# Two attention-fed MoE layers on one Trainium2 core: converting float64 weights with two VectorE operations, an in-place rebias and three load buffers

## The chip, the cores and the metric

The kernel runs on one core of a Trainium2 chip. Its five engines work side by side, each on its own in-order list of instructions: TensorE (PE in the profile; its weight loads are PEld), VectorE (DVE), ScalarE (ACT), GpSimd (POOL), and SyncE (SP), which here only issues transfers. The metric is the device time of one execution in microseconds, as a median over runs.

## The reference, cut to what matters

Attention over 4 batches of 576 tokens, 8 heads of 64: a pooled part (four neighbouring tokens averaged) plus a banded part. Its output x (2304 tokens by 512) goes through two MoE layers. The weights of both layers arrive as float64.

```
x   = attention(q, k, v)                                  # float32
x   = (sigmoid(x @ w_gate) * (x @ w_val)) @ w_out         # MoE 1: 512 -> 1536 -> 512
h   = x @ w2_in                                           # MoE 2: 512 -> 2048 -> 512
out = (h * tanh(log(1 + exp(h)))) @ w2_out                # float32
```

## The kernel before

The program treats the four batches in turn. While TensorE multiplies batch b in MoE 1 (`m1` and `m1out`, lines 846 and 875), the attention of batch b+1 is woven in between, so all engines have work of both. MoE 2 follows for all tokens at the end.

**Weights.** MoE 1 has 18 units of weights (12 for the first products, 6 for the second), each fetched in two halves of 128 x 512 float64 words. They are converted once, in the block of batch 0, written to DRAM as float32 (`wd`, lines 228 and 256), and read back from there for batches 1 to 3. One half goes through these steps:

- `load64` (line 169): SyncE issues the load of the raw words (512 KB) into a `raw` tile of 128 x 512 x 2 int32. There are two `raw` buffers.
- `narrow` (line 176): a double's high word is read as a float32 and rebiased by ScalarE (line 178) into a tile of its own, `rebias` (two buffers of 128 x 512). VectorE then has three operations: shift that left by three (line 180, one source), OR in the top three bits of the low word (line 181, two sources), OR in the sign (line 185, two sources).
- `split` (line 189): ScalarE rounds the float32 to float32r (line 190), and GpSimd, or VectorE in some places, subtracts to get the rest (line 191). TensorE multiplies with both parts.

`d`, the float32 tile, holds a whole unit and has two buffers.

**What orders the work.** The first batch's attention, with the first three units, is written out by hand in `ORDER`, where `wf`, `wn` and `ws` are fetch, narrow and split of a half. All later steps are laid by `weave` (line 792) on a modelled TensorE clock: a step is emitted once those it depends on lie far enough back. In block 0 the fetch of half (u, x) depends on the narrowing of (u - 1, x), two halves before (line 271). The narrowing `wp` (line 242, `part`) comes at least 6000 ns of that clock after its fetch, and at least 2100 ns after the half before. The matmuls' slots need the splits of their unit, and a unit needs its place in a ring of three.

MoE 2's weights pass through `narrow` too: 16 halves of `w2_out` (`narrow_steps`, blocks 1 and 2) and 16 of `w2_in` (block 3). In MoE 2 itself the activation (`mish_a`) keeps its tile `e` in the `raw` buffers, and the output (`finish`, line 1097) passes through the `rebias` buffers.

Of the kernel before, what the change touches and what calls it, by code (L numbers as in the profile page):

```python
# [8 lines left out]
F32 = mybir.dt.float32  # L9
F32R = mybir.dt.float32r  # L10
I32 = mybir.dt.int32
AF = mybir.ActivationFunctionType
# [5 lines left out]
# the first batch's loads and steps in the order of their issue  # L18
ORDER = [['k0a', 'k0c', 'k1a', 'k1c', 'q0a', 'q0c', 'v1a', 'v1c', 'w0', 'q1c', 'v0c', 'w2', 'v0a',
# [11 lines left out]
# the engines of those steps, and how far apart the second batch's steps are laid (ns)  # L31
# [17 lines left out]
def attn_moe_kernel(  # L49
# [30 lines left out]
    T2 = 256  # L80
# [5 lines left out]
    def subs(b):  # L86
        """The two parts of the tokens of batch b that the products of MoE 1 take in turn."""
        a = 2 * TQ if b == 0 else SUB
        return slice(0, a), slice(a, S)
# [10 lines left out]
    class Step:  # L100
        """A piece of a program: what emits it, the time it takes of the tensor engine, and
        what has to lie how far back on the tensor engine's clock."""
# [5 lines left out]
    # ---------------------------------------------------------------- memory  # L108
# [21 lines left out]
    # the products of MoE 1 come to lie where the first batch's rows are gone  # L130
# [37 lines left out]
    # ------------------------------------------------- float64 words to float32  # L168
    def load64(src, n):
        r = fpool.tile([128, 512, 2], I32, tag="raw", name="raw")  # L170
        SP.dma_start(
            out=r.rearrange("p (a b) z -> p a (b z)", a=n), in_=src.bitcast(I32)
        )
        return r

    def narrow(r, d):
        g = fpool.tile([128, 512], F32, tag="rebias", name="rebias")
        ACT.activation(out=g, in_=r[:, :, 1].bitcast(F32), func=AF.Copy, scale=2.0 ** -112)  # L178
        gi, di = g.bitcast(I32), d.bitcast(I32)
        DVE.tensor_scalar(out=di, in0=gi, scalar1=3, scalar2=None, op0=ALU.logical_shift_left)  # L180
        DVE.scalar_tensor_tensor(  # L181
            out=di, in0=r[:, :, 0], scalar=29, in1=di,
            op0=ALU.logical_shift_right, op1=ALU.bitwise_or,
        )
        DVE.scalar_tensor_tensor(  # L185
            out=di, in0=gi, scalar=SIGN, in1=di, op0=ALU.bitwise_and, op1=ALU.bitwise_or
        )
# [5 lines left out]
    # ------------------------------------------------------- weights of MoE 1  # L193
# [15 lines left out]
    def weights(b):  # L209
        """The steps that bring the units of block b on chip and split them."""  # L210
# [52 lines left out]
        for u in range(NU1):  # L263
            for x in range(2):
# [5 lines left out]
                if b == 0:  # L270
                    deps = [(("wp", b, u - 1, x), 0.0)]
# [15 lines left out]
    # ------------------------------------------------------------- attention  # L287
# [3 lines left out]
    def windows(i):  # L291
        """Of tile i: first query, first key, first row used and rows used, for its halves."""
# [8 lines left out]
    def attention(b):  # L301
# [43 lines left out]
        # the first batch's rows lie where the products of MoE 1 come later, four neighbouring  # L345
        # tokens of half the sequence to a partition
# [110 lines left out]
        # pooled attention, half the queries at a time; heads in the order (parity, pair)  # L457
# [39 lines left out]
        # the same for half of the pairs, with the transposes  # L497
# [68 lines left out]
        # banded attention, two windows of 64 queries by 64 keys at a time  # L566
# [225 lines left out]
    def weave(slots, steps):  # L792
        """Emits the slots in their order, and the steps among them: each once what it stands
        on lies far enough back, and the paced ones evenly by cost."""
# [44 lines left out]
    # ----------------------------------------------------------------- MoE 1  # L839
# [6 lines left out]
    def m1(b, f, sub):  # L846
# [14 lines left out]
        # sigmoid(a) = (1 + tanh(a / 2)) / 2; the last half comes with the second product  # L861
# [13 lines left out]
    def m1out(b, c2, fg, j, ps):  # L875
# [19 lines left out]
        if fg == last_g:  # L895
            if b == B - 1 and c2:
                # the ring is free but for its last unit
# [12 lines left out]
    def block(b, extra):  # L910
        """MoE 1 of batch b with the steps of `extra` woven in."""
# [29 lines left out]
    # ------------------------------------------------------- weights of MoE 2  # L941
# [224 lines left out]
```

## Time and profile before

| what | value |
| --- | --- |
| runs | 1068.31, 1070.77, 4706.45 us; median 1070.77 us |
| span of the profiled execution, first to last instruction | 1069.6 us |
| what the median has beyond that span | 1.2 us |
| TensorE busy | 1023.1 us (96%) |
| VectorE busy | 690.6 us (65%) |
| ScalarE busy | 521.3 us (49%) |
| GpSimd busy | 195.2 us (18%) |
| mean granted TensorE clock | 0.987 of full |

The profile gives no time of the profiled execution other than its span; it lies between the two lowest runs. A share of busy time is a mean over stages with different limits: here the first 300 us (attention of batch 0, block 0, start of block 1) differ from the rest. A TensorE that is busy is not one at its peak, since matmuls overlap and the granted clock may be low.

### The profile page before, as it was taken

The numbers are of one execution on the slowest core, as the hardware profiler recorded it, in microseconds if no ns is written. First come the engines' busy times: TensorE is split into PE (matmuls) and PEld (weight loads), VectorE is DVE, ScalarE is ACT, GpSimd is POOL, SyncE is SP. The second block draws the span as 40 slices with busy tenths as digits, with TensorE's granted clock in tenths as the row PEclk, the third lists the DMA queues.
The fourth block names the chain that finished last, engine by engine and source line by source line (L and its number), as shares of the span: only waits on it lengthen the run. The fifth ranks groups of instructions, "written<-read, shape, count | busy, mean of one in ns | idle before, by whom it ended". The sixth has DMA issues, their size and how long they took to land.

```text
span 1069.6 us, 20453 instructions
## 1 busy us (share of the span) xinstructions
PE 1023.1 (96%) x8152; PEld 956.0 (89%) x8152; DVE 690.6 (65%) x1107; ACT 521.3 (49%) x1222; POOL 195.2 (18%) x235
## 2 busy tenths in 40 slices
PE   4698988999999999999999999999999999999998
PEld 3588978899999999899999999999999999999997
DVE  6977988856975537955488931867555555555552
ACT  4654657346665437565356631654443443433432
POOL 6456564630400400400000002000000000000000
PEclk9998998999999999999999999999999999999999
DMA  8639665777752457622375548212112020220001
GB/s 199 174 103 238 178 204 189 220 241 237 220 184 60 135 179 227 212 101 61 124 243 182 173 167 264 65 29 59 23 37 60 1 60 5 56 60 1 21 1 40
DMA packets 122240, 134.51 MB, mean 126 GB/s; under 512 B 54432, under 2 KB 99488, under 8 KB 122144
## 3 DMA queue, kind: packets, MB, share of 16 engines
q1 hardware_dynamic: 110336, 115.37, 35.1%
q0 software_dynamic: 11808, 17.83, 6.2%
q8 instruction: 64, 1.05, 0.4%
q14 instruction: 32, 0.26, 0.1%
HBM read 101.19 MB, written 31.98 MB: 124 GB/s over the span
## 4 chain that ended last, share of the span: by engine, by line
PE 77%; DVE 11%; DMA 6%; ACT 3%; issue 2%; SPq 0%; POOL 0%; DVEq 0%; ACTq 0%
PE ps_m L857 7%; PE ps_m L859 7%; PE ps_m L858 7%; PE h L1060 6%; PE h L1062 6%; PE h L1061 6%; PE po L1070 6%; PE po L1068 6%; PE po L1069 6%; PE ps_o L888 5%; PE ps_o L890 4%; PE ps_o L892 4%; DVE d L181 2%; DMA raw<-in_moe_w_out_dram 2%; DVE d L185 2%
## 5 line engine op out<-in xcount | busy, mean ns | idle before, releaser
L857 PE MATMUL ps_m<-R 128*128 128x288 f32 (+2 forms) x768 | 236.0, 309 | 4.2 <-DVE sg L863 4.2
L858 PE MATMUL ps_m<-R 128*128 128x288 f32 (+2 forms) x768 | 232.5, 303 | 0.8 <-POOL R L191 0.8
L859 PE MATMUL ps_m<-R 128*128 128x288 f32 (+2 forms) x768 | 232.7, 303 | 0.5 <-POOL R L191 0.5
L857 PEld LDWEIGHTS ps_m<-R 128*128 128x128 f32 x768 | 148.4, 194 | 9.6 <-DVE sg L863 4.6
L190 ACT CAST R<-d 128x512 fp32r<-128x512 f32 (+1 forms) x192 | 108.6, 583 | 89.2 <-PE ps_o L890 34.4
L858 PEld LDWEIGHTS ps_m<-R 128*128 128x128 f32 x768 | 148.8, 194 | 1.9 <-POOL R L191 1.0
L859 PEld LDWEIGHTS ps_m<-R 128*128 128x128 f32 x768 | 148.6, 194 | 1.7 <-POOL R L191 0.9
L191 DVE TENSOR_TENSOR R<-d,R 128x512 fp32r<-128x512 f32 (+1 forms) x158 | 105.5, 682 | 55.1 <-ACT R L190 52.9
L888 PE MATMUL ps_o<-G,R 128*128 128x288 f32 (+2 forms) x384 | 116.5, 303 | 0.0
L890 PE MATMUL ps_o<-G,R 128*128 128x288 f32 (+2 forms) x384 | 114.4, 298 | 0.0
L892 PE MATMUL ps_o<-G,R 128*128 128x288 f32 (+2 forms) x384 | 114.2, 298 | 0.0
L1068 PE MATMUL po<-R,G 128*128 128x512 f32 (+1 forms) x247 | 94.5, 383 | 0.0
L1069 PE MATMUL po<-R,G 128*128 128x512 f32 (+1 forms) x247 | 94.0, 381 | 0.0
L1070 PE MATMUL po<-R,G 128*128 128x512 f32 (+1 forms) x247 | 93.5, 383 | 0.0
L1081 ACT ACTIVATE e<-e 128x1024 f32<-128x1024 f32 (+1 forms) x48 | 40.6, 846 | 107.2 <-DVE e L1080 107.2
L1062 PE MATMUL h<-R 128*128 128x256 f32 x320 | 90.2, 282 | 0.0
L1061 PE MATMUL h<-R 128*128 128x256 f32 x320 | 90.2, 282 | 0.0
L1060 PE MATMUL h<-R 128*128 128x256 f32 x320 | 90.2, 282 | 0.0
L1080 DVE TENSOR_SCALAR e<-h 128x1024 f32<-128x1024 f32 (+1 forms) x48 | 45.9, 956 | 58.3 <-PE h L1062 58.1
L178 ACT ACTIVATE rebias<-raw 128x512 f32<-128x512 f32 x68 | 46.0, 677 | 59.8 <-DMA raw<-in_moe_w_out_dram 23.5
L888 PEld LDWEIGHTS ps_o<-G,R 128*128 128x128 f32 x384 | 72.9, 190 | 1.2
L890 PEld LDWEIGHTS ps_o<-G,R 128*128 128x128 f32 x384 | 73.0, 190 | 0.1
(126 smaller groups left out, 2290.3 us busy)
## 6 DMA issues: line engine op xcount, KB each, us to landing
d<-wd SPq DMA_DIRECT2D x54, 512.0 KB
raw<-in_moe_w_out_dram SPq DMA_DIRECT2D x28, 512.0 KB
wd<-d SPq DMA_DIRECT2D x18, 512.0 KB
wd<-R SPq DMA_DIRECT2D x32, 256.0 KB
raw<-in_moe_w_in_dram SPq DMA_DIRECT2D x16, 512.0 KB
x2d<-R SPq DMA_DIRECT2D x24, 288.0 KB
R<-wd POOLq DMA_DIRECT2D x13, 512.0 KB, 6.9
raw<-in_moe_w_gate_dram SPq DMA_DIRECT2D x12, 512.0 KB
```

Of the source, the lines that this page charges most:

```text
L857: PE.matmul(p[:, 0:n], lhsT=wh, rhs=xh[:, c, ts], start=(c == 0), stop=False)
L858: PE.matmul(p[:, 0:n], lhsT=wh, rhs=xl[:, c, ts], start=False, stop=False)
L859: PE.matmul(p[:, 0:n], lhsT=wl, rhs=xh[:, c, ts], start=False, stop=(c == KD - 1))
L888: PE.matmul(p[:, 0:n], lhsT=hi[:, o:o + 128], rhs=gt[:, f, 0, ts], start=(f == 0), stop=False)
L890: PE.matmul(p[:, 0:n], lhsT=hi[:, o:o + 128], rhs=gt[:, f, 1, ts], start=False, stop=False)
L892: PE.matmul(p[:, 0:n], lhsT=lo[:, o:o + 128], rhs=gt[:, f, 0, ts], start=False, stop=(f == KF1 - 1))
L1060: PE.matmul(o, lhsT=wi[:, 0, c, cs], rhs=x[:, 0, c, :], start=(c == 0), stop=False)
L1061: PE.matmul(o, lhsT=wi[:, 0, c, cs], rhs=x[:, 1, c, :], start=False, stop=False)
L1062: PE.matmul(o, lhsT=wi[:, 1, c, cs], rhs=x[:, 0, c, :], start=False, stop=(c == KD - 1))
L1068: PE.matmul(p, lhsT=g[:, 0, ts], rhs=w[:, 0, cs], start=(j == 0), stop=False)
L1069: PE.matmul(p, lhsT=g[:, 0, ts], rhs=w[:, 1, cs], start=False, stop=False)
L1070: PE.matmul(p, lhsT=g[:, 1, ts], rhs=w[:, 0, cs], start=False, stop=(j == KF2 - 1))
```

## The change

- `narrow`: the rebias is written back into the high words of the raw tile, so the `rebias` tile is gone. ScalarE has a second operation: it reads the top byte of each low word (one byte in eight), multiplies by 1/32, adds 1/64 - 1/2 and writes the rounded integer, which is the top three bits, to `d`. VectorE's first operation is now (rebiased word shifted left by three) OR `d`; its second, the sign, is as before but reads the raw tile. The one-source shift (line 180) is gone.
- `raw` has three buffers instead of two. 3 x 4 KB take the place of 2 x 4 KB and 2 x 2 KB.
- In block 0 a fetch depends on the narrowing three halves before (`NRAW = 3`) instead of two.
- In `ORDER` the fetches of the first units move forward: `wf.1.0` to just after `wf.0.1` and `ga.0`, `wf.1.1` to just after `wn.0.0`, `wf.2.0` to just after `wn.0.1`, `wf.2.1` to just after `wn.1.0`.
- `mish_a` and `finish` share the three `raw` buffers.

```diff
     def load64(src, n):
-        r = fpool.tile([128, 512, 2], I32, tag="raw", name="raw")
+        r = fpool.tile([128, 512, 2], I32, tag="raw", bufs=NRAW, name="raw")
...
     def narrow(r, d):
-        g = fpool.tile([128, 512], F32, tag="rebias", name="rebias")
-        ACT.activation(out=g, in_=r[:, :, 1].bitcast(F32), func=AF.Copy, scale=2.0 ** -112)
-        gi, di = g.bitcast(I32), d.bitcast(I32)
-        DVE.tensor_scalar(out=di, in0=gi, scalar1=3, scalar2=None, op0=ALU.logical_shift_left)
+        g = r[:, :, 1].bitcast(F32)
+        ACT.activation(out=g, in_=g, func=AF.Copy, scale=2.0 ** -112)
+        gi, di = r[:, :, 1], d.bitcast(I32)
+        ACT.activation(
+            out=di, in_=r.bitcast(U8)[:, :, 3], func=AF.Copy, scale=1.0 / 32, bias=1.0 / 64 - 0.5
+        )
         DVE.scalar_tensor_tensor(
-            out=di, in0=r[:, :, 0], scalar=29, in1=di,
-            op0=ALU.logical_shift_right, op1=ALU.bitwise_or,
+            out=di, in0=gi, scalar=3, in1=di, op0=ALU.logical_shift_left, op1=ALU.bitwise_or
         )
...
                 if b == 0:
-                    deps = [(("wp", b, u - 1, x), 0.0)]
+                    deps = [(("wp", b) + divmod(2 * u + x - NRAW, 2), 0.0)]
...
-            e = fpool.tile([128, 4 * T2], F32, tag="raw", name="e")[:, 0:n]
+            e = fpool.tile([128, 4 * T2], F32, tag="raw", bufs=NRAW, name="e")[:, 0:n]
...
-            o = fpool.tile([128, DM], F32, tag="rebias", name="o")
+            o = fpool.tile([128, DM], F32, tag="raw", bufs=NRAW, name="o")
```

## Rows read from the trace of the kernel before

**Rows 1.** Busy time by stage; bracket is the count; then clock, DMA share, GB/s
```profile
core 0: us, PE busy (x) PEld busy (x) DVE busy (x) ACT busy (x) POOL busy (x), PEclk, DMA share, GB/s
20.00:51.40 31.40, 19.18 (x212) 15.85 (x213) 30.37 (x55) 19.21 (x69) 18.64 (x26) 1.00 0.71 194
75.00:95.00 20.00, 19.16 (x199) 18.39 (x195) 14.27 (x19) 9.16 (x18) 14.99 (x20) 1.00 0.79 202
95.00:207.00 112.00, 100.98 (x894) 93.06 (x893) 101.03 (x156) 66.24 (x202) 67.80 (x61) 0.91 0.67 203
300.00:432.00 132.00, 131.55 (x1261) 125.11 (x1260) 78.91 (x173) 74.23 (x238) 14.63 (x26) 1.00 0.49 153
660.00:1070.00 410.00, 406.14 (x2636) 370.13 (x2635) 225.64 (x241) 171.43 (x212) 13.28 (x20) 1.00 0.15 41
```

**Rows 2.** Groups by line on VectorE, 95 to 207 us: busy, mean ns, idle before
```profile
L185 DVE SCALAR_TENSOR_TENSOR d<-rebias,d 128x512 int32<-128x512 int32 x25 | 25.4, 1015 | 0.3
L181 DVE SCALAR_TENSOR_TENSOR d<-raw,d 128x512 int32<-128x512 int32 x24 | 21.3, 889 | 0.2
L180 DVE TENSOR_SCALAR d<-rebias 128x512 int32<-128x512 int32 x24 | 15.6, 651 | 5.2 <-ACT rebias L178 3.9 <-issue 1.3
```

**Rows 3.** Groups by line on ScalarE, 95 to 207 us
```profile
L178 ACT ACTIVATE rebias<-raw 128x512 f32<-128x512 f32 x24 | 16.2, 675 | 16.0 <-DMA raw<-in_moe_w_val_dram 7.7 <-DMA raw<-in_moe_w_out_dram 6.6 <-DMA raw<-in_moe_w_gate_dram 1.5
L190 ACT CAST R<-d 128x512 fp32r<-128x512 f32 x22 | 13.6, 617 | 9.6 <-DVE d L185 9.6
```

**Rows 4.** Chain that ended last, 93 to 115 us: start, duration, what
```profile
93.85 2.96 DVE d L185
...
96.83 0.62 ACT R L190
97.45 0.49 ACT qT L414
...
97.99 1.12 PE ps_l L579 x16
```

**Rows 5.** Busy time by engine just behind that stall (columns of rows 1)
```profile
98.00:102.00 4.00, 4.00 (x30) 3.68 (x31) 1.27 (x4) 3.94 (x20) 3.77 (x7) 0.50 0.96 295
```

**Rows 6.** Timelines of GpSimd and VectorE, 38 to 42 us: start, duration
```profile
38.42 1.31 POOL L191 TENSOR_TENSOR R<-d,R 128x512 fp32r<-128x512 f32 x1 [0.80 <-ACT R L190]
...
38.52 1.50 DVE L180 TENSOR_SCALAR d<-rebias 128x512 int32<-128x512 int32 x1
40.05 0.69 DVE L181 SCALAR_TENSOR_TENSOR d<-raw,d 128x512 int32<-128x512 int32 x1
...
41.39 0.42 DVE L180 TENSOR_SCALAR d<-rebias 128x512 int32<-128x512 int32 x1
41.72 0.63 DVE L674 TENSOR_TENSOR xn<-ps_la,od 128x464 f32<-128x464 f32 x1
```

**Rows 7.** Timeline of ScalarE, 44 to 46 us
```profile
44.57 0.69 ACT L178 ACTIVATE rebias<-raw 128x512 f32<-128x512 f32 x1 [0.91 <-DMA raw<-in_moe_w_gate_dram]
45.16 0.61 ACT L190 CAST R<-d 128x512 fp32r<-128x512 f32 x1
```

**Rows 8.** Chain that ended last, just ahead of the first matmuls of MoE 1
```profile
48.34 0.93 DVE d L185
49.27 0.55 DVE xn L674
```

**Rows 9.** Line 180 alone on VectorE, 20 to 51.4 us: busy time and count
```profile
20.00:51.40 31.40, 5.11 (x6) 1.00 0.71 194
```

**Rows 10.** Chain that ended last, around one late load
```profile
138.77 6.11 DMA raw<-in_moe_w_val_dram
144.90 0.68 ACT rebias L178
```

**Rows 11.** Who waited for whom on VectorE, 90 to 225 us: total, times, longest
```profile
DVE d L180 <- POOL R L191: 4.1, 1, 4.1
```

**Rows 12.** Timeline of TensorE, 98 us: its idle time before and who ended it
```profile
97.99 1.12 PE L579 MATMUL ps_l<-kT,qT 64*64 64x64 f32 x16 [2.35 <-ACT qT L414]
```

More of the change, by code (lines that the diff above doesn't have):

```diff
@@ L11 @@
 I32 = mybir.dt.int32
+U8 = mybir.dt.uint8
 AF = mybir.ActivationFunctionType
@@ L17 @@
 SIGN = -2147483648
-ORDER = [['k0a', 'k0c', 'k1a', 'k1c', 'q0a', 'q0c', 'v1a', 'v1c', 'w0', 'q1c', 'v0c', 'w2', 'v0a',
[3 rows of a table removed]
+ORDER = [['k0a', 'k0c', 'k1a', 'k1c', 'q0a', 'q0c', 'v1a', 'v1c', 'w0', 'q1c', 'v0c', 'w2', 'v0a', 'w1',
[3 rows of a table added]
     'ls.1.0', 'vd.4', 'ls.1.1', 'le.1', 'gn.0.0', 'gt.0.0', 'ln.0', 'gn.0.1', 'vd.7', 'wf.0.0',
[7 rows of a table removed]
[7 rows of a table added]
 ENG = {'L.t0': 3000, 'L.t': 420, 'L.vd': 3750, 'L.vd0': 1800, 'L.pool': 1600, 'L.ls': 4500, 'L.s1':
@@ L166, in attn_moe_kernel @@
     x2d = dram.tile([128, 2, KD, NT], F32, name="x2d")
+    NRAW = 3
     def load64(src, n):
-        r = fpool.tile([128, 512, 2], I32, tag="raw", name="raw")
+        r = fpool.tile([128, 512, 2], I32, tag="raw", bufs=NRAW, name="raw")
         SP.dma_start(
```

20 rows, old and new, of the table ORDER are left out of this document.

## The prediction

> **What bounds the kernel now.** I read the page first: TensorE is busy for 96% of the span, which says little about where a change to VectorE and ScalarE could matter. So I cut the span by stage [rows 1]. The reader is to see two kinds of stage. From 300 us on TensorE is full: 131.55 of 132 us, and 406.14 of 410 us in MoE 2. Nothing done to VectorE there can be worth more than the few microseconds it idles. From 20 to 51.4 us VectorE is busy for 30.37 of 31.4 us while TensorE works for 19.18. From 95 to 207 us VectorE is busy for 101.03 of 112 us, TensorE idles for 11.0 us, and its granted clock is 0.91. These two are the stages to argue about.
>
> Then the groups of VectorE in that long stage [rows 2]: three operations of `narrow` take 25.4 + 21.3 + 15.6 = 62.3 of its 101.03 us. The chain of waits shows how that reaches TensorE [rows 4]: line 185 takes 2.96 us, the cast on ScalarE waits for its result, the copy of qT stands behind that cast in ScalarE's queue, and TensorE waits for qT. Behind this gap the granted clock is 0.50 for 4 us [rows 5], the lower of its two levels (1.2 instead of 2.4 GHz), so a stall is paid about twice.
>
> **The change part by part.** All sums are made against the span of 1069.6 us; the median run is 1.2 us above it, so I take what I gain off 1070.8.
>
> *The shift (line 180) goes.* Free of others it takes 0.42 us, and the next instruction starts 0.33 us after it began (41.39 to 41.72) [rows 6]. In the long stage its mean is 651 ns, 15.6 us for 24 [rows 2]. The surplus is a wait for GpSimd: the shift that began at 38.52, 0.1 us behind a GpSimd subtraction, took 1.50 us and ended 0.3 us after the subtraction [rows 6]. The two-source operations suffer as well (889 and 1015 ns against 0.69 alone) [rows 2, 6]. So if the shift is gone, the next one may stand in the same place and wait instead. From below 24 x 0.33 = 7.9 us are freed, from above 15.6. I take 10, nearer the lower end, since the rows show two-source operations held longer than the shift.
>
> The Trainium skill, "SBUF — State Buffer", section "Who interferes with whom", says that VectorE in a two-port mode or with two SBUF inputs and GpSimd exclude each other for a whole instruction, and that the second to issue fully blocks. The durations in rows 6 agree. By that rule alone the wait passes to the next operation and the term would be 7.9; by a rule that only the one-source shift is locked it would be 15.6.
>
> *ScalarE gets a second operation.* The trace has none with byte input; the nearest row is line 178 with the same count and stride, 0.69 us, with the next start 0.59 us later [rows 7]. Bounds: the cast's mean of 0.617 us [rows 3] and twice that row, 1.4 us, should the in-place strided write or the byte read be slow. I take 0.59 per half, 24 x 0.59 = 14.2 us in the long stage. ScalarE is busy there for 66.24 of 112 us, so it goes to about 80. Its cover is this idle time; what it idles for is in part the late load, 7.7 + 6.6 + 1.5 = 15.8 us in front of line 178 [rows 3], and the third buffer aims at just that. If the cover is gone, the 14.2 us stand on the chain.
>
> *Loads three halves ahead.* A load issued at 138.77 landed 6.11 us later and ScalarE waited for it [rows 10]. 24 halves in 112 us are 4.7 us per half, so a fetch that hangs on the narrowing one half earlier is issued some 4.7 us sooner, more than most of those waits: 15.8 us for 24 halves are 0.7 on average. No bytes are added, and the DMA share in the stage is 0.67 [rows 1]. What is gained is not the 15.8 (ScalarE is not the bound), but a part of the 112 - 101 = 11 us in which VectorE idles, of which 3.9 stand before line 180 as a wait for the rebias [rows 2]. I take 3; bounds 0 and 11.
>
> *Waits added.* ScalarE's new operation writes `d`, so it now waits for the buffer's last readers, which VectorE did before; one such wait took 4.1 us [rows 11]. Behind it in ScalarE's queue stand the tanh, the casts and the copies for which TensorE waits. ScalarE also works in longer runs: in rows 5 it is busy for 3.94 of 4 us already. I set 2 us for both; bounds 0 and the 14.2 of above. SyncE's queue gets the moved fetches of the first units earlier; a fetch ahead of its buffer would hold what is behind it, but three buffers serve three fetches, and later ones stand behind the narrowing that frees them. I set 0; the cover is that the DMA share there is 0.71 [rows 1], and if it goes, one load like that in rows 10 is late, 6 us.
>
> *The start.* The first matmuls of MoE 1 come at the end of the stage that VectorE fills. The addition xn of the second tile stands right behind line 185 [rows 8], and behind five of the six shifts [rows 9]. Removing five gives 5 x 0.33 = 1.7 us from below and about 5.1 from above. I take 2.5, as above nearer the lower end. ScalarE idles for 12.2 us here, which covers 5 x 0.59 = 3.0.
>
> *75 to 95 us*: TensorE idles 0.84 us [rows 1]; I take 0.5. *From 300 us on*, the 32 halves of MoE 2's weights and the shared buffers of `e` and `o`: 0, covered by a full TensorE; at most 410 - 406.1 = 3.9 us idle are in play in MoE 2, either way.
>
> Sum: 2.5 + 0.5 + (10 + 3 - 2) = 14. 1070.8 - 14 = 1056.8, so 1057.
>
> **The rivals.** *All of VectorE's debt goes.* TensorE's floor in the long stage is its busy time less what the low clock cost: 0.09 x 112 = 10.1 us, plus 11.0 idle, so at most 21.1 are to be had. With 5.1 at the start and 2 around it the time is 1042.6. For it: VectorE's operations stand directly on the chain, and stalls cost double [rows 4, 5]. Against it: lines 181 and 185 keep 46.7 us, held by GpSimd, which stays busy for 67.8 us.
>
> *The waits only pass on.* The next operation is blocked by GpSimd in the shift's stead, and TensorE's in-order list of attention steps sets the pace. Then the start's 1.7 and perhaps 2 us in the stage are left, 1067. For it: waits like those of rows 6 fall to whoever comes. It is also what comes out if the weave still lays a unit's narrowing by the ring of three, so that fetching early starts nothing earlier.
>
> *ScalarE becomes the bound, and it gets slower.* Place: the new operation in front of tanh, cast and qT copy, waiting for `d`. Price: such a wait, held through to TensorE, costs a gap as the one behind rows 4, 2.35 us [rows 12], and 2.0 for the 4 us at half clock that follow [rows 5], 4.35 together. From 14 / 4.35 = 3.2 such stalls on nothing is gained; five make it 1070.8 - 14 + 21.8 = 1078.6. For it: rows 5, ScalarE full in a burst. Against it: VectorE paid the buffer wait only once at that length before.
>
> The Trainium skill, "ScalarE: Activation LUTs", section "Rules for kernel authors", advises VectorE rather than ScalarE for plain arithmetic, because it is faster per element; the change does the reverse, and here the rows agree on the speeds (0.42 against 0.69). By that rule the slower engine takes the chain, and this rival's 1079 would come out; the trace speaks against it only in that VectorE, not ScalarE, is the full one.
>
> **How the numbers follow.** Forecast 0.53; all debt gone 0.22; waits pass on 0.17; slower 0.08. A difference of 2%, 21.4 us, is about what a measurement of this kernel can tell from no change. Faster by that much means below 1049: the second case and the forecast's tail, 0.24. Slower by that much, above 1092, needs 35 / 4.35 = 8 stalls: 0.02. The rest, 0.74, is within. The range runs from 1041 (floor reached) to 1072 (waits pass on, 1067, and one more stall of 4.35); beyond it lie most of the slower case and little else.
>
> **What would show it.** Right: line 180 is gone and VectorE has two operations per half whose means are no longer than before; a second ScalarE line of about 0.65 to 0.7 us per half; ScalarE's waits for raw loads in block 0 at less than half; TensorE idle in the stage that was 95 to 207 us under 6 us with a clock above 0.94; the first MoE 1 matmul about 2 us sooner. Wrong: VectorE's two remaining operations grow by what the shift lost (waits pass on); TensorE's gaps end on ScalarE with VectorE idle (ScalarE the bound); new gaps behind 300 us, in MoE 2's activation, would be a cost that I set at nothing.

## The result and the profile after

The changed kernel takes 1083.40 us (median of 14 runs, 1077.97 to 1088.20), against 1073.32 us for the kernel before, taken beside it. The ratio is 1.0093, with a 95% interval of 1.0071 to 1.0115. It is slower by about 10 us, where 14 us faster were forecast.

The profiled execution has a span of 1083.9 us, 14.3 us more than that of the profile before. That is more than the 10 us of the medians, since the profile before is of one of its fastest runs and the one after of a run 2.3 us above its median. Where the 14.3 us lie is read from the start of the last copy of MoE 1's output (`ps_o`) in each block, which closes the work of that batch. In block 0, before and after:

```profile
244.24 0.46 ACT L902 ACTIVATE R<-ps_o 128x344 fp32r<-128x344 f32 x1
```

```profile
249.62 0.46 ACT L908 ACTIVATE R<-ps_o 128x344 fp32r<-128x344 f32 x1
```

All stretches:

| stretch | before, us | after, us | difference |
| --- | --- | --- | --- |
| start to first matmul of MoE 1 | 51.4 | 51.7 | +0.3 |
| from there to the end of block 0 | 192.8 | 197.9 | +5.1 |
| block 1 | 150.1 | 156.0 | +5.9 |
| block 2 | 156.9 | 158.9 | +2.0 |
| block 3 | 108.3 | 108.1 | -0.2 |
| MoE 2 | 410.0 | 411.2 | +1.2 |

The same windows as in [rows 1], of the changed kernel. The ends are moved where its stages end later, and 52 to 95 us is new (columns of rows 1).

```profile
20.00:51.40 31.40, 18.23 (x206) 15.08 (x206) 26.94 (x52) 23.37 (x77) 19.81 (x27) 0.88 0.77 214
52.00:95.00 43.00, 38.11 (x404) 34.29 (x404) 27.24 (x54) 20.15 (x51) 22.94 (x30) 0.85 0.58 145
75.00:95.00 20.00, 17.79 (x196) 16.48 (x197) 9.58 (x14) 8.13 (x15) 12.82 (x20) 0.92 0.71 181
95.00:212.00 117.00, 108.26 (x981) 100.71 (x981) 89.63 (x136) 80.19 (x231) 65.98 (x65) 0.94 0.69 198
300.00:432.00 132.00, 128.93 (x1216) 122.20 (x1215) 75.12 (x163) 71.76 (x220) 12.53 (x24) 0.97 0.49 151
673.00:1083.00 410.00, 406.84 (x2640) 371.01 (x2640) 224.92 (x241) 170.67 (x213) 13.35 (x20) 1.00 0.15 41
```

VectorE lost work, as forecast: 26.94 instead of 30.37 us in the start, 89.63 of 117 instead of 101.03 of 112 us in the long stage. ScalarE gained it, 80.19 instead of 66.24. Nothing became shorter by that. The row to stop at is 52 to 95 us: TensorE has 404 matmul records there at a clock of 0.85; the same window before has 447 at 1.00. The loss begins in a stretch for which the forecast had 0.5 us of gain.

Groups by line on VectorE and ScalarE, 95 to 212 us of the changed kernel (columns of rows 2 and 3). Lines 181, 185, 188, 191 and 196 are the rebias, the low bits, VectorE's two operations and the cast; the GpSimd subtraction is line 197.

```profile
L188 DVE SCALAR_TENSOR_TENSOR d<-raw,d 128x512 int32<-128x512 int32 x24 | 24.2, 1022 | 8.0 <-ACT d L185 8.0
L191 DVE SCALAR_TENSOR_TENSOR d<-raw,d 128x512 int32<-128x512 int32 x24 | 21.6, 911 | 0.1
...
L181 ACT ACTIVATE raw<-raw 128x512 f32<-128x512 f32 x25 | 17.0, 679 | 20.1 <-DMA raw<-in_moe_w_out_dram 10.9 <-DMA raw<-in_moe_w_val_dram 5.4 <-DMA raw<-in_moe_w_gate_dram 3.6
L185 ACT ACTIVATE d<-raw 128x512 int32<-128x512 uint8 x24 | 15.7, 666 | 0.8 <-DMA wd<-d 0.7
```

Three things are to be seen. The operations cost about what was forecast: the low bits 666 ns; VectorE's first operation 1022 ns where line 181 took 889, and its second 911 ns where line 185 took 1015 [rows 2], together 1933 against 1904. The waits for raw loads did not fall: 20.1 us against 16.0 [rows 3], in spite of three buffers. And ScalarE hardly idles in front of its new operation (0.8 us), yet VectorE waits 8.0 us for its result: the operation is not held at the head of ScalarE's queue; it stands late in it.

### The profile page after: what moved, and what is told of

Same layout as the page of the kernel before. It is cut to its first block, busy times and chain, and to the rows that moved or that the text cites. A ratio compares the mean times of both kernels' runs of the same rounds, so it can differ in the third digit from the quotient of the medians.

```text
span 1083.9 us, 20416 instructions
## 1 busy us (share of the span) xinstructions
PE 1027.0 (95%) x8152; PEld 959.5 (89%) x8152; DVE 654.7 (60%) x1039; ACT 556.8 (51%) x1290; POOL 188.8 (17%) x235
## 4 chain that ended last, share of the span: by engine, by line
PE 76%; DMA 8%; DVE 7%; ACT 4%; issue 2%; POOL 1%; SPq 1%; ACTq 0%; DVEq 0%; POOLq 0%
PE ps_m L863 7%; PE h L1066 6%; PE h L1068 6%; PE h L1067 6%; PE ps_m L865 6%; PE ps_m L864 6%; PE po L1076 6%; PE po L1074 6%; PE po L1075 6%; PE ps_o L894 5%; PE ps_o L896 4%; PE ps_o L898 4%; DMA wd<-R 2%; DVE R L197 2%; PE ps_l L585 1%
## 5 line engine op out<-in xcount | busy, mean ns | idle before, releaser
L181 ACT ACTIVATE raw<-raw 128x512 f32<-128x512 f32 x68 | 46.1, 678 | 56.9 <-DMA raw<-in_moe_w_out_dram 29.1
L894 PEld LDWEIGHTS ps_o<-G,R 128*128 128x128 f32 x384 | 73.1, 190 | 1.2
L188 DVE SCALAR_TENSOR_TENSOR d<-raw,d 128x512 int32<-128x512 int32 x68 | 59.1, 876 | 24.3 <-ACT d L185 23.8
```

Of the source, the lines that this page charges most:

```text
L894: PE.matmul(p[:, 0:n], lhsT=hi[:, o:o + 128], rhs=gt[:, f, 0, ts], start=(f == 0), stop=False)
```

## The experiments

Four theories were on the table at first. A: ScalarE's new operation writes `d` and so waits for that buffer in ScalarE's in-order queue. B: the fetches that were moved forward disturb other loads. C: ScalarE's added work itself costs. D (later): two raw buffers, or another order, explain a fast run. Theory G came out of the traces and is told below. All times stand beside runs of the kernel before on the same chip (1072.8 to 1074.4 us); "block 0" is the start of its last copy of MoE 1's output in the profile (244.24 before, 249.62 after).

**e1: the old order of fetches** (`ORDER` of before, and):

```diff
-                    deps = [(("wp", b) + divmod(2 * u + x - NRAW, 2), 0.0)]
+                    deps = [(("wp", b) + divmod(2 * u + x - 2, 2), 0.0)]
```

> The changed narrow with three load buffers, but the fetches ordered as before (two halves ahead, the old list for the first batch). Theory A (ScalarE's new operation writes d, so it waits in ScalarE's queue for the readers of d, which in the changed kernel's profile is 15.7 us in 13 waits): nothing changes, 1079 to 1086 us, and those waits stay at 12 us or more. Theory B (the fetches moved forward hold SyncE's queue and make batch 1's loads late): the time of before, 1070 to 1076, and the first tok loads of batch 1 are back from 84.9 to about 78 us. Theory C (ScalarE simply has too much to do): as A.

Measured: 1085.08 us, ratio 1.0094 (1.0061 to 1.0126), block 0 at 249.27. As slow as the changed kernel: the moved fetches are not what costs here. B falls as the cause of this loss.

**e2: three operations on VectorE again**, in place, three raw buffers, new fetches:

```diff
-        ACT.activation(
-            out=di, in_=r.bitcast(U8)[:, :, 3], func=AF.Copy, scale=1.0 / 32, bias=1.0 / 64 - 0.5
-        )
+        DVE.tensor_scalar(out=di, in0=gi, scalar1=3, scalar2=None, op0=ALU.logical_shift_left)
         DVE.scalar_tensor_tensor(
-            out=di, in0=gi, scalar=3, in1=di, op0=ALU.logical_shift_left, op1=ALU.bitwise_or
+            out=di, in0=r[:, :, 0], scalar=29, in1=di,
+            op0=ALU.logical_shift_right, op1=ALU.bitwise_or,
         )
```

> The old three VectorE operations on a raw tile rebiased in place, with three buffers and the fetches three halves ahead, so ScalarE has no second operation. Theory A: the loss goes, 1065 to 1075, for nothing on ScalarE waits for d. Theory B: the loss stays, 1080 to 1086. Theory C: the loss goes, as in A. The part of my prediction on early loads would show as a gain of some 3 us below 1073.

Measured: 1082.82 us, ratio 1.0078 (1.0055 to 1.0101). Slow without any second operation on ScalarE: neither A nor C expects that. The time lies where B put it, against e1; e6 and e11 take it apart.

**e3: low bits into the raw tile**, in the place of the low words, instead of `d`:

```diff
-            out=di, in_=r.bitcast(U8)[:, :, 3], func=AF.Copy, scale=1.0 / 32, bias=1.0 / 64 - 0.5
+            out=r[:, :, 0], in_=r.bitcast(U8)[:, :, 3], func=AF.Copy, scale=1.0 / 32, bias=1.0 / 64 - 0.5
...
-            out=di, in0=gi, scalar=3, in1=di, op0=ALU.logical_shift_left, op1=ALU.bitwise_or
+            out=di, in0=gi, scalar=3, in1=r[:, :, 0], op0=ALU.logical_shift_left, op1=ALU.bitwise_or
```

> The changed kernel, but ScalarE writes the low three bits back into the raw tile's low words instead of into d; VectorE's first operation reads them there. ScalarE does the same work and has no wait for d; that wait is VectorE's again. Theory A: most of the loss goes, 1066 to 1076. Theory B: stays at 1080 to 1086. Theory C (ScalarE's load): stays at 1080 to 1086.

Measured: 1067.64 us, ratio 0.9947 (0.9928 to 0.9966), block 0 at 233.82. The same instructions, one with another place to write to, and 16 us less than the changed kernel. C falls as the cause of the loss; A is borne out so far.

**e4: the same with the old fetches** (the two edits above together).

> As the run before, with the old order of the fetches as well. Theory A: as the run before, 1066 to 1076, within 4 us of it. Theory B alone: 1070 to 1076. Theory C: 1080 to 1086. If both A and B hold in part this is the fastest of the four.

Measured: 1068.63 us, ratio 0.9952 (0.9929 to 0.9975), block 0 at 234.48. The answer does not hang on the order of fetches.

**e5: three `d` buffers, two raw buffers, old fetches; low bits in `d`** (`NRAW = 2`, `bufs=3` on `d`):

> The changed narrow (ScalarE writes d), fetches as before, but the third buffer goes to d instead of to the raw tile. Theory A (ScalarE's wait for the readers of d costs the time): with a third d the wait is all but gone without touching the operations, 1066 to 1076, and its row is under 4 us. Rival S (what the other runs gained is the luck of another instruction order, not that wait): anywhere from 1068 to 1088, with the wait's row saying nothing about it.

Measured: 1066.47 us, ratio 0.9941 (0.9914 to 0.9968), block 0 at 247.21. Fast, but not as expected: the wait of line 185 for line 197 was still 13.1 us, all of it in blocks 1 to 3, and block 0 did not get shorter.

**e6 and e11: three operations in place, old fetches, with three and with two raw buffers** (the edits of e1 and e2; e11 also `NRAW = 2`).

> Three VectorE operations in place, three raw buffers, fetches as before. The run with the new fetches was 1083, though nothing on ScalarE waited for d. If the early fetches cost that (they hold SyncE's queue), this one is at 1070 to 1076. If the rebias in place costs it (the raw tile is held until the third operation instead of the second), it stays at 1080 to 1086.

> Three VectorE operations in place with two raw buffers and fetches as before: of the kernel before, only the tile of the rebias (and the output's tile in MoE 2) differ. If the rebias in place is what costs: 1080 to 1088, at least as slow as with three buffers. If it is the third buffer or the fetch: 1070 to 1076.

Measured: 1079.39 us, ratio 1.0045 (1.0020 to 1.0070), and 1076.70 us, ratio 1.0040 (1.0018 to 1.0062). Each lies between its two expectations and meets neither. The in-place rebias (with the tile for MoE 2's output, which went with it) costs some 0.4%, and the third raw buffer gives three operations nothing.

**e8: low bits in raw with two raw buffers, old fetches** (e4 and `NRAW = 2`).

> The low bits in the raw tile, two VectorE operations, two raw buffers, fetches as before. If the third buffer is worth something to this form, 1071 to 1078 (3 to 10 us slower than with three); if it is worth nothing, 1066 to 1071.

Measured: 1077.79 us, ratio 1.0024 (0.9999 to 1.0048), block 0 at 247.98. Against e4 the third buffer is worth 1077.79 - 1068.63 = 9.2 us here. With e6 and e11 this makes a square, all with old fetches: taking the shift off VectorE gives nothing clear with two raw buffers (e11 to e8, 1.0040 to 1.0024), the third buffer gives nothing to three operations (e11 to e6, 1.0040 to 1.0045), and the two together give 0.9% (e11 to e4, 1.0040 to 0.9952).

**e10: e5 without its third `d` buffer** (old fetches, `NRAW = 2`, nothing else changed).

> The changed conversion with two raw buffers and the old order of fetches: the earlier run with three d buffers without the third d buffer, nothing else. Theory A (ScalarE's low-bits operation waits in ScalarE's in-order queue for the float32 tile d, above all in block 0): the gain of that run over the kernel before (ratio 0.994) goes, and the time is 1080 to 1090 us against about 1073 for the kernel before (ratio 1.006 to 1.015). Theory D (that run was quick by its two raw buffers or by its order, not by d): it stays at 1066 to 1070 us (0.993 to 0.997).

Measured: 1075.10 us, ratio 1.0012 (0.9996 to 1.0028), block 0 at 246.27. Theory D misses; A misses too, for it expected 1080 or more. Of the variants with two operations so far, only those with three raw buffers and low bits in `d` together are slow: with two raw and two `d` buffers there is no clear loss. The third `d` buffer of e5 is worth 8.6 us, but not in block 0.

**e13 and e14: low bits in raw for the 36 halves of block 0 alone, and for the 32 of MoE 2's weights alone.**

```diff
-    def narrow(r, d):
+    def narrow(r, d, low=False):
...
+        li = r[:, :, 0] if low else di
...
-                        narrow(raws.pop((u, x)), d[:, cs])
+                        narrow(raws.pop((u, x)), d[:, cs], True)
```

> The changed kernel, but in block 0 and ahead of it (36 halves) ScalarE's low bits go into the raw tile, in the place of the low words; the 32 halves of MoE 2's weights still write them to their own float32 tile, of which there is one buffer. Theory A0 (the buffer that costs is the d of block 0): 1067 to 1071 us, ratio 0.994 to 0.998, about all that the low bits in raw gave everywhere (1067.6). Theory A1 (it is the single tile of MoE 2's weights, where the trace shows the wait of line 185 for GpSimd's line 197): 1079 to 1084 us (1.005 to 1.010).

> The counterpart: low bits in the raw tile only for the 32 halves of MoE 2's weights in blocks 1 to 3; the 36 halves of block 0 write them to d. Theory A0: no help, 1079 to 1084 us (ratio 1.005 to 1.010). Theory A1: 1067 to 1071 us (0.994 to 0.998). If both halves of the pair gain about half (1074 to 1077 each), both buffers cost.

Measured: 1071.40 us, ratio 0.9991 (0.9971 to 1.0011), block 0 at 235.06, just above A0's range and far below A1's; and 1080.19 us, ratio 1.0070 (1.0045 to 1.0095), block 0 at 251.72, as A0 said. With e3 and the changed kernel this is a square: block 0's low bits are worth 1.0% and 1.2%, those of MoE 2's weights 0.2% and 0.4%. The place is block 0.

**e12: no low bits at all.** ScalarE has the rebias alone; VectorE's first operation takes the rebiased words twice, so the low three bits are left out and the words are not those of the weights; the time alone is of interest.

```diff
-        ACT.activation(
-            out=di, in_=r.bitcast(U8)[:, :, 3], func=AF.Copy, scale=1.0 / 32, bias=1.0 / 64 - 0.5
-        )
         DVE.scalar_tensor_tensor(
-            out=di, in0=gi, scalar=3, in1=di, op0=ALU.logical_shift_left, op1=ALU.bitwise_or
+            out=di, in0=gi, scalar=3, in1=gi, op0=ALU.logical_shift_left, op1=ALU.bitwise_or
         )
```

> The variant with low bits in raw, without ScalarE's second operation at all: the low three bits are left out, and VectorE's first operation takes the rebiased words as its second source, so VectorE's work is the same. It prices the operation itself once its wait for d is gone. Theory A (the operation runs beside other work and only its wait for d costs): within 3 us of the variant that has it (1067.6), so 1065 to 1069. Theory B2 (ScalarE's 45 us of added work also stand on the chain in part): 1055 to 1062 us.

Measured: 1071.59 us, ratio 0.9987 (0.9968 to 1.0006), outside both expectations: 4 us more than e3, which has 68 operations of 0.67 us more on ScalarE. So that work is not what limits e3. The run does not price the operation itself, though, for it laid the instructions in another order: its block 0 ends at 242.63, against 233.82 in e3. It warns how far a difference of 4 us may be read.

### Where the changed kernel and e3 part

The two traces have the same order of matmuls until 65 us, where four transposes (line 526) start at 65.45 us in e3 and at 66.30 in the changed kernel. So the question is what differs around there. Timeline of VectorE in the changed kernel, its conversions and the subtraction of the second tile:

```profile
64.20 1.31 DVE L188 SCALAR_TENSOR_TENSOR d<-raw,d 128x512 int32<-128x512 int32 x1
...
66.07 0.68 DVE L191 SCALAR_TENSOR_TENSOR d<-raw,d 128x512 int32<-128x512 int32 x1
...
71.65 0.78 DVE L188 SCALAR_TENSOR_TENSOR d<-raw,d 128x512 int32<-128x512 int32 x1 [0.96 <-ACT d L185]
72.46 1.05 DVE L191 SCALAR_TENSOR_TENSOR d<-raw,d 128x512 int32<-128x512 int32 x1
...
81.98 0.63 DVE L197 TENSOR_TENSOR R<-xn,R 128x448 fp32r<-128x448 f32 x1 [0.63 <-ACT R L196]
82.52 1.29 DVE L188 SCALAR_TENSOR_TENSOR d<-raw,d 128x512 int32<-128x512 int32 x2
```

VectorE in e3, and below it in the kernel before (whose lines 191 and 180 are the subtraction and the shift); neither has any conversion from 58 us to the rows shown:

```profile
76.96 0.63 DVE L197 TENSOR_TENSOR R<-xn,R 128x448 fp32r<-128x448 f32 x1 [1.03 <-ACT R L196]
77.50 3.67 DVE L188 SCALAR_TENSOR_TENSOR d<-raw 128x512 int32<-128x512 int32 x3
```

```profile
78.28 0.63 DVE L191 TENSOR_TENSOR R<-xn,R 128x448 fp32r<-128x448 f32 x1 [1.03 <-ACT R L190]
78.83 2.82 DVE L180 TENSOR_SCALAR d<-rebias 128x512 int32<-128x512 int32 x2
```

The conversions that stand right behind the subtraction are held there by a rule in `part` (lines 252 and 253 before): for unit 3, the first that is not in `ORDER`, what `narrow` puts on that subtraction's engine, VectorE, is issued behind it. Its two halves keep VectorE free for the second tile's attention. The rule names unit 3 alone. Unit 4 was held all the same, by the buffers: unit 3's two halves kept both raw tiles until the rule let them go.

The change took both holds away. The third raw tile lets half 8, the first of unit 4, be loaded. And `d` is now first written by ScalarE, which the rule does not bind: the low bits of units 3 and 4 take the two `d` tiles ahead of the subtraction. ScalarE in the changed kernel (63.49 is half 8; 70.42 and 70.98 are half 9, the second of unit 4, told apart by the order of the loads):

```profile
63.49 0.68 ACT L185 ACTIVATE d<-raw 128x512 int32<-128x512 uint8 x1
...
70.42 0.66 ACT L181 ACTIVATE raw<-raw 128x512 f32<-128x512 f32 x1 [0.60 <-DMA raw<-in_moe_w_val_dram]
70.98 0.64 ACT L185 ACTIVATE d<-raw 128x512 int32<-128x512 uint8 x1
...
71.80 0.68 ACT L98 COPY ETg<-ps_gt 72x288 f32<-72x288 f32 x2
```

So unit 4's conversion is ready at 64 us and lands in VectorE's attention steps, ahead of unit 3's, which the rule holds until 82.52. In e3, where VectorE is the first to write `d`, unit 4's conversion comes behind unit 3's, and the third operation in "x3" is unit 4's, behind the rule. What it does to TensorE, in the changed kernel:

```profile
69.87 0.77 PE L561 MATMUL ps_ga<-ETg,vd 72*64 72x72 f32 x16 [1.04 <-ACT ETg L98]
72.24 0.50 PE L561 MATMUL ps_ga<-ETg,vd 72*64 72x72 f32 x2 [1.60 <-ACT ETg L98]
72.67 1.12 PE L654 MATMUL ps_lt<-ident,El 128*128 128x128 f32 x4
...
85.70 0.42 PE L864 MATMUL ps_m<-R 128*128 128x344 f32 x1 [2.21 <-POOL R L197]
```

and in e3:

```profile
69.42 0.34 PE L561 MATMUL ps_ga<-ETg,vd 72*64 72x72 f32 x2 [0.31 <-ACT ETg L98]
69.69 0.66 PE L654 MATMUL ps_lt<-ident,El 128*128 128x128 f32 x4
...
80.68 0.42 PE L864 MATMUL ps_m<-R 128*128 128x344 f32 x1 [2.03 <-POOL R L197]
```

Two gaps of 1.04 and 1.60 us, then the four transposes of line 654 take 1.12 instead of 0.66 us, and the first product of the second part starts at 85.70 instead of 80.68: 5.0 us behind. The first gap goes back to VectorE: behind its conversion of 64.20 the attention's reductions come later, an operation of ScalarE on their result (line 633) starts at 68.90 instead of 67.08, and the copy of ETg stands behind that. The second gap ends on the copy of 71.80, which stands in ScalarE's list behind the rebias and the low bits of half 9, and that rebias had waited 0.60 us for its load. So here ScalarE's own conversion steps are in the way too.

The windows around and behind the second gap (changed kernel) show the rest:

```profile
70.00:75.00 5.00, 3.40 (x37) 2.63 (x37) 3.62 (x7) 2.61 (x7) 2.03 (x2) 0.64 0.07 10
75.00:80.00 5.00, 5.00 (x88) 4.39 (x90) 2.92 (x7) 2.25 (x4) 3.65 (x7) 0.67 0.70 220
```

The clock is 0.64 and 0.67 there, partly at the lower of its two levels; e3 has 1.00 in both windows. It pays later: from 81 to 85 us its clock is 0.57, behind the gap of 2.03 us.

Most of the loss comes after that. Counted in order, the matmuls of MoE 1's products (into `ps_m` and `ps_o`, 3456 in each trace) lag behind those of e3 by 3.5 us at the 101st (89.48 against 85.97 us), by 11.2 at the 171st (110.50 against 99.27), by 9.9 at the 701st (215.94 against 206.07) and by 16.3 at the 751st (233.22 against 216.91). The window in which the lag grows most, in the changed kernel and below it in e3:

```profile
95.00:111.00 16.00, 11.61 (x94) 10.52 (x94) 11.27 (x13) 9.10 (x19) 13.59 (x16) 0.83 1.05 238
```

```profile
95.00:111.00 16.00, 16.00 (x144) 15.28 (x142) 14.26 (x19) 11.64 (x36) 10.85 (x12) 1.00 1.10 257
```

TensorE idles 4.4 us of these 16 in the changed kernel, at a clock of 0.83; in e3 it is full. Which late step holds it there was not taken apart; this is what precedes it on ScalarE in the changed kernel:

```profile
77.83 0.69 ACT L181 ACTIVATE raw<-raw 128x512 f32<-128x512 f32 x1 [1.21 <-DMA raw<-in_moe_w_gate_dram]
...
96.38 0.68 ACT L181 ACTIVATE raw<-raw 128x512 f32<-128x512 f32 x1 [4.64 <-DMA raw<-in_moe_w_val_dram]
...
98.07 0.66 ACT L185 ACTIVATE d<-raw 128x512 int32<-128x512 uint8 x1 [0.67 <-DMA wd<-d]
```

The rebias of 77.83 gets its low bits only at 98.07, since units 3 and 4 own both `d` tiles; all that while its raw tile stays full. The load of the half behind it is issued at 90.44 (in e3 at 88.15), and ScalarE idles 4.64 us for it. For line 185 up to 260 us, who waited for whom:

```profile
L185 ACT ACTIVATE d<-raw x38: 642/664/692, 31.3 to 257.8; 128x512 int32<-128x512 uint8 x38
...
who waited for it (us, times):
  DVE d L188: 16.6, 12
```

In e3 the same row says 5.9 us, 8 times. A second loss stands at the end of block 0 (chain of the changed kernel that ended last):

```profile
193.09 4.42 DVE d L188
...
199.19 4.85 DMA araw<-in_v_dram
...
204.63 2.60 POOL vd L434 x3
207.25 0.33 SPq L331
...
208.11 7.34 DMA raw<-in_moe_w_out_dram
...
222.40 0.79 DVE El L642
...
223.32 1.09 PE ps_lt L654 x4
```

SyncE's queue holds a raw load (line 174) behind a transfer for the attention (line 331) that waits for GpSimd. The load is issued at 208.11, three conversions stand behind it on VectorE, and TensorE idles 6.3 us for line 642. Before, that wait is 2.1 us; in e1 and e14, where unit 4 comes first too, 5.9 and 4.8; in e3 2.2. But e2 and e6 have it as well, 6.4 and 7.1 us, with their units in order, so this second loss is not shown to come from the order of the units.

This is theory G, and it says what A does not: the rule, widened to unit 4, should mend it, with the low bits still in `d`.

**e16: the rule widened to unit 4**, the changed kernel otherwise; **e17: the same with e1's old fetches.**

```diff
-                        if u == NRING:
+                        if u in (NRING, NRING + 1):
```

> The changed kernel with one condition widened: VectorE's conversions of unit 4 are queued behind the same subtraction of the second tile's attention as those of unit 3 (before, unit 3 alone). Low bits still go to d, three raw buffers, same loads, same operations. Theory G (with the third raw buffer, and with d handed out by ScalarE's low-bits operation which that rule does not hold, unit 4's conversion slips in front of unit 3's and into VectorE's part of the attention at 64 to 73 us; the delay and the disorder of units cost the loss): block 0 ends at 234 to 240 us and the time is 1066 to 1073 us, ratio 0.993 to 1.000. Theory A (ScalarE's operation standing between a freed d and VectorE costs, all through block 0): block 0 ends at 246 to 252 us, 1079 to 1085 us (1.005 to 1.011).

> The same widened condition with the order of fetches of the kernel before (the earlier run with old fetches: 1085.1 us, ratio 1.009), so that the answer does not hang on one order. Theory G: 1066 to 1074 us (0.993 to 1.001). Theory A: 1079 to 1086 us (1.005 to 1.012).

Measured: e16 1075.53 us, ratio 1.0018 (0.9999 to 1.0037), block 0 at 239.11; e17 1070.33 us, ratio 0.9966 (0.9948 to 0.9985), block 0 at 237.25. VectorE, TensorE and ScalarE in e16:

```profile
76.44 0.62 DVE L197 TENSOR_TENSOR R<-xn,R 128x448 fp32r<-128x448 f32 x1 [1.04 <-ACT R L196]
76.98 3.67 DVE L188 SCALAR_TENSOR_TENSOR d<-raw,d 128x512 int32<-128x512 int32 x3
```

```profile
69.17 0.66 PE L654 MATMUL ps_lt<-ident,El 128*128 128x128 f32 x4
```

```profile
239.11 0.46 ACT L908 ACTIVATE R<-ps_o 128x344 fp32r<-128x344 f32 x1
```

One condition takes back 10.5 us of block 0 in the one order of fetches and 12.0 in the other, and in the runs 0.75% and 1.28% of the time, 8 and 14 us. e16's block end lies where G put it (for e17 none was stated), and e17's time does; e16's time lies 2.5 us above G's range and 3.5 below A's. Over the whole run line 185 waits as long for the last readers of its tile in e16 as in the changed kernel, 15.7 against 16.4 us, so what A blames is still there and most of the loss is not. e16 stays 0.7% behind e3, while e17 lies within the interval of e4: here the moved fetches cost 0.5% (e17 to e16), though they cost nothing between e4 and e3 or between e1 and the changed kernel. Why was not settled.

**e22: e3 without the rule.**

```diff
-                    with ExitStack() as behind:
-                        if u == NRING:
-                            behind.enter_context(tc.issue_after(splits[ENG['gate']]))
-                        narrow(raws.pop((u, x)), d[:, cs])
+                    narrow(raws.pop((u, x)), d[:, cs])
```

> The variant with low bits in raw (1067.6 us, ratio 0.995) without the rule that queues unit 3's conversions behind that subtraction: VectorE and ScalarE take units 3 and 4 as soon as they are loaded. Theory G (conversions let into VectorE's part of the attention cost several us): slower than with the rule by 4 to 12 us, 1072 to 1080 us (0.999 to 1.007), with TensorE's progress at 95 us behind. Theory A says nothing of that rule: 1065 to 1071 us (0.993 to 0.998).

Measured: 1085.16 us, ratio 1.0101 (1.0069 to 1.0132), block 0 at 253.40: 17.5 us slower than e3, more than G expected, with no low bits in `d`. VectorE and TensorE in e22:

```profile
63.89 0.69 DVE L188 SCALAR_TENSOR_TENSOR d<-raw 128x512 int32<-128x512 int32 x1 [1.75 <-ACT raw L185]
...
66.15 0.68 DVE L188 SCALAR_TENSOR_TENSOR d<-raw 128x512 int32<-128x512 int32 x1
```

```profile
72.51 1.12 PE L651 MATMUL ps_lt<-ident,El 128*128 128x128 f32 x4
```

The same picture as in the changed kernel, conversions among the attention steps at 64 to 68 us and transposes at 1.12 us, without the one thing that theory A blames. And the units are in order in e22: halves 6 to 9 are converted at 51.90, 55.45, 63.89 and 66.15 us. So conversions among the attention steps are enough; the disorder of the units, the other half of G, is not needed for the loss.

The 171st matmul of MoE 1's products, counted as above, sorts all variants. The four with conversions of unit 4 ahead of the subtraction (the changed kernel, e1, e14, e22) lag there 8.7 to 13.0 us behind e3; the other eleven lie between 3.4 us ahead of it and 2.3 us behind. A falls as the main cause, and G's first half is shown from both sides.

### What G does not explain

Block ends are from one profiled execution each, which need not be a typical one: e5's is its slowest run, 7 us above its median, and e13's its fastest, 6 us below. Over all variants, block 0's last copy lies at 249.3 to 253.4 us where unit 4 is converted among the attention steps (after, e1, e14, e22). With two operations, three raw tiles and the conversions behind the subtraction it lies at 233.8 to 239.1 (e3, e4, e13, e16, e17); e12, of the same form, lies at 242.6, which is not explained. With two raw tiles and two operations it lies at 246.3 to 248.0 (e5, e8, e10), and with three operations at 247.8 to 251.6 (e2, e6, e11). These six keep up with e3 until 111 us and lose later: theirs is another loss, and which was not settled.

Nor is the loss of 5.9 + 2.0 us in blocks 1 and 2. It is there in e3 as well (4.5 and 2.1 us) and in e16 (3.2 and 3.1), so it does not come from unit 4. In blocks 1 and 2 of the changed kernel TensorE waits 4.4 us for line 498 of the attention; the kernel before has 0.6 there. But e5 has 4.2 us of that wait, and its blocks 1 and 2 take 306.9 us together, as before (307.0). In e5, with its third `d` buffer, block 1 is 147.2 us long against 152.9 in e10, which is most of what that buffer gives. A hint lies in three pairs that differ in the third raw tile alone: with it, blocks 1 and 2 together are 4.6 (e11 to e6), 4.7 (e8 to e4) and 3.7 us (e10 to e1) longer. Yet e13, which differs from e3 only in where MoE 2's low bits go, is 4.2 us shorter than e3 there, so single executions do not settle it. No run took these blocks apart.

Four variants beat the kernel before: e5 (0.9941), e3 (0.9947), e4 (0.9952) and e17 (0.9966); the smallest edit of the changed kernel among them is e3's two operands.

## Why the prediction was wrong

- *The shift goes, -10 us.* Right only together with the third raw tile and the old place of unit 4: e3's block 0 ends 10.4 us earlier than before, against 10 + 3 - 2 + 0.5 = 11.5 forecast for this term and those around it. With two raw tiles the shift gives nothing clear (e11 to e8: block 0 at 247.76 and 247.98 us). The sum added this term and the next but one as if each stood by itself.
- *ScalarE's second operation, hidden.* Right: 666 ns against the 0.59 to 0.69 taken from [rows 7], 80.19 us busy against "about 80", and leaving it out (e12) made nothing faster. It is not hidden everywhere: the second gap at 72 us stands behind it. The Trainium skill, "ScalarE: Activation LUTs", section "Rules for kernel authors", prefers VectorE for additions and multiplications. By that rule alone the move to ScalarE would be the loss; e6 to e4, where three operations on VectorE become two and one on ScalarE and the ratio falls from 1.0045 to 0.9952, disagrees.
- *Loads three halves ahead, -3 us.* The third raw tile is worth 9.2 us with units in order (e8 to e4) and costs 1085.08 - 1075.10 = 10 us with low bits in `d` (e10 to e1). Issuing the loads earlier gives nothing in either form (e4 to e3, e1 to the changed kernel). The forecast priced the tile alone; its sign hangs on who writes `d` first.
- *Waits added, +2 us, at most 14.2.* This is the step that failed. It saw that "ScalarE's new operation writes `d`", and priced that as waits at the head of ScalarE's queue, on the instruction order of before. Such waits are 0.7 us in block 0, and 15.7 us in blocks 1 to 3, where e16 has them too without the loss. What moved was the right to the buffer: ScalarE, now the first writer, takes the tile, the rule on VectorE's list no longer held unit 4, and the order itself changed. The runs price that at 8 us (after to e16) and 14 us (e1 to e17), and 17.5 where the rule goes altogether (e3 to e22).
- *The start, -2.5 us.* Missed: VectorE is busy 3.4 us less there, and the first matmul comes at 51.7 instead of 51.4. In e3 it is 51.6. A sum of busy time did not set that end.
- *From 300 us on, 0.* A second step that failed: blocks 1 and 2, for which a full TensorE was to cover everything, are 7.9 us longer, more than half of the 14.3 (6.6 us in e3, 6.3 in e16). The cause stays open. MoE 2 is 1.2 us longer, within the 3.9 allowed.
- *The rivals.* "ScalarE becomes the bound" forecast 1079 and comes nearest, in the main by luck. Its place is seen once, in the second gap at 72 us, but ScalarE is not full (80 of 117 us), the first gap is VectorE's, and five stalls of 4.35 us are not what is seen. The price of a stall was right in kind: 2.6 us of gaps at 69 and 72 us became 5.0 us by 85.70. "All debt goes" did not happen. "Waits pass on" is not seen in the changed kernel's means, 1933 ns for the two operations against 1904; with two raw tiles, where the shift's absence gives nothing clear (e8), it was not tested.

## What to carry to other kernels

When an operation moves to another engine, ask which engine is now the first to write each tile: a hold put on one engine's list reaches the others only through buffers that are not yet free, and a moved first writer or one buffer more can undo it. Price a change on the order of instructions that it leads to, not on the old one: look for the first instruction that changes its place and for what it stands in front of. Where a buffer is added, name what its scarcity was holding back. And price two gains together as well as one by one: here neither the missing shift nor the third buffer gave anything clear without the other.

## What the runs showed of the hardware

- A read of one byte in eight with a scale and a bias, written as int32, costs ScalarE as much as the strided float operation of the same count: 666 against 679 ns for 128 x 512. Writing it back in strides of 8 bytes (e3) takes 667 ns, so in these rows neither stride nor type shows.
- Around TensorE's gaps of 1.04 and 1.60 us in the changed kernel the granted clock is 0.64 from 70 to 75 us and 0.67 from 75 to 80, with four transposes at 1.12 instead of 0.66 us. A gap's length alone does not foretell this: behind the gap of 2.03 us in e3 the clock is 0.57 from 81 to 85 us, and behind the gap of 2.21 us in the changed kernel it is 1.00 from 85.7 to 90.
- The Trainium skill, "SBUF — State Buffer", section "Who interferes with whom", says that a VectorE instruction with two SBUF inputs contends with a GpSimd instruction that reads SBUF. Nothing here is against it: beside GpSimd the two operations left take 1022 and 911 ns on the average, where one took 0.69 us alone [rows 6]. With the shift gone the two take together 1933 ns in the changed kernel, 1993 in e3 and 1874 in e4, against 1904 before: little of the shift's 651 ns passed on to them.
